# The first piece of wo as loads of 112 and 16 partitions, with the last 6 KB of the 16 in threes

## The chip, the cores and the metric

The kernel runs on one core of a Trainium2 chip. TensorE (PE) multiplies, VectorE (DVE), ScalarE (ACT) and GpSimd (POOL) work beside it, and SyncE (SP) issues most of the transfers between the memory outside (HBM) and the on-chip memory SBUF of 128 partitions. Sixteen DMA engines carry the transfers. The time is the device time of one execution in microseconds (us); comparisons use the median of several executions of each kernel.

## The reference

One token is decoded. Attention with 32 query heads and 8 key heads over a cache of 32768 positions is mixed by a gate with a gated feed-forward block:

```
q = x @ wq                                   # 32 heads of 128
p = softmax(q k^T / sqrt(128)); o = p v      # 8 key heads, 4 queries each, 32768 positions
a = o.reshape(1, 4096) @ wo                  # wo: 4096 x 512
b = (silu(x @ w1) * (x @ w3)) @ w2           # 512 -> 1792 -> 512
out = g * a + (1 - g) * b,   g = sigmoid(sum(x * gate_w))
```

All is float32. The two caches are 128 MB each, so nearly all of the time is their reading.

## The kernel before, in words

Two buffers of 64 KB a partition, big_a and big_b, take the caches turn by turn in units of 8 MB: 16 units of keys, then 16 of values with a lag of four. PE computes scores from transposed keys and products with values, DVE transposes the keys and finds the softmax's maxima and sums, ACT copies a part of each key unit into the tile aside and takes the exponentials.

The order of the work is written out in the program. A small class (Program) keeps, for each engine, a list of operations with the keys that each one reads and writes; from these it works out on which semaphore an operation must wait. The function load (L195) puts a transfer on SP's list. Each such load takes one of nine semaphores in turn (its lane), so a load waits until the load that used the lane nine loads earlier has landed. SP issues its list in order, and all that SP issues stands in one queue (q1) of the 16 DMA engines.

What matters here is the end. The last four units of values are loaded into big_a and big_b (load_unit, L592 to L603), then w2 into the tile aside (L604). As soon as PE has used the third of those units (values at L606), big_a is free, and SP issues wo into it in six pieces (L608 to L610). wo is seen as 128 partitions x 32 rows of 512 numbers: a partition has 32 contiguous rows of 2 KB, 64 KB in all. The six pieces are rows 0 to 16, 16 to 23, 23 to 27, 27 to 29, 29 to 31 and 31 to 32 of every partition, that is 32, 14, 8, 4, 4 and 2 KB a partition.

Meanwhile PE does the last unit of values, DVE folds in w2 by parts (down, L635), and the attention's result is laid out in otp (L644). Then PE multiplies by wo. The first three pieces are used by "wide" products, one group for each piece (L650, recorded at L630), each waiting for its own piece; DVE adds their sum to acc (L652). The last three are used by products of 128 columns (L661), which also take in acc. A copy (L673) and two stores (L504) end the kernel.

Of the kernel before, what the change touches and what calls it, by code (L numbers as in the profile page):

```python
# [13 lines left out]
P = 128  # L14
# [104 lines left out]
def kernel(  # L119
# [13 lines left out]
    nc = tc.nc  # L133
# [23 lines left out]
    pr = Program(nc, tc.alloc_semaphore)  # L157
# [12 lines left out]
    wo_t = big[0].rearrange("p (k e) -> p k e", k=32)  # L170
# [15 lines left out]
    otp = kt[1][:, 0:1024].rearrange("p (k c) -> p k c", c=32)  # L186
# [8 lines left out]
    def load(dst, src, writes, over=()):  # L195
        lanes[0] += 1
        lane = f"load{lanes[0] % 9}"
        return pr.add(
            "SP", lambda: nc.sync.dma_start(dst, src), writes=writes, over=[*over, lane], inc=lane, by=16, also=lane,  # L199
        )  # L200
# [81 lines left out]
    for c in range(NC):  # L282
        def part(c=c):
# [18 lines left out]
         reads=["gate0"], writes=["gate1"])  # L302
# [39 lines left out]
    def window(t, z):  # L342
        return act(
            lambda: A.copy(winc, win[:, t // 4, :, 16 - 16 * z:48 - 16 * z]),  # L344
            reads=[("win", t // 4, r) for r in range(4)], writes=["winc"], credit="windows",
        )
# [162 lines left out]
    first = window(0, 0)  # L509
    for t in range(NH):  # L510
# [9 lines left out]
        if t + 1 < NH:  # L520
            load_keys(t + 1)
            first = window(t + 1, 0)
# [83 lines left out]
        values(7, 0, z, region(0, z), f"A{z}")  # L606
    wod = wo.rearrange("(p k) e -> p k e", k=32)
    parts = ((0, 16), (16, 23), (23, 27), (27, 29), (29, 31), (31, 32))  # L608
    for a, b in parts:
        load(wo_t[:, a:b, :], wod[:, a:b, :], [("wo", a)], over=["A0", "A1"])  # L610


# [13 lines left out]
    def wide(i, ws, **kw):  # L626
        def go():
            for j, (w, t) in enumerate(ws):
                r = 32 * (j % 4)
                ins = T.matmul(pa[r:r + 32, :], w, t, start=(i == 0 and j < 4), stop=(final[j % 4] == (i, j)))  # L630
            return ins
        pe(go, writes=["f0"], **kw)


    def down(ks):  # L635
# [9 lines left out]
        reads=[("each", 0), ("each", 1), "otp"], writes=["lay"])  # L645
# [2 lines left out]
    down(range(3, FR))  # L648
    laid = ["otp", "lay"]
    for i, (a, b) in enumerate(parts[:3]):  # L650
        wide(i, [(otp[:, k, :], wo_t[:, k, :]) for k in range(a, b)], reads=[*laid, ("wo", a)])
    dve(lambda: V.tensor_add(acc, acc, pa), reads=["acc", "f0"], writes=["acc"])  # L652


# [27 lines left out]
    a, b, c, d = flips  # L682
# [67 lines left out]
```

## Time and profile before

| | us |
|---|---|
| time, median of 3 runs | 693.98 (693.81 to 694.11) |
| the profiled execution, from first to last instruction (its span, the one time that the page gives of it) | 692.4 |
| PE busy | 402.8 |
| DVE busy | 368.4 |
| ACT busy | 134.6 |
| data moved by DMA | 296.34 MB at a mean of 428 GB/s |

The profile is of one execution. Its page gives busy times, the span in 40 slices, the DMA queues, and the chain of work that ended last. Further views give the instructions in order of time (the timeline), the list of DMA issues with the time to landing, and, for any stretch of the span, the busy time of each engine, the granted clock of PE, the busy share of the 16 DMA engines and their rate. A DMA's packets are counted by queue; q1 is SP's, q10 is ACT's.

### The profile page before, as it was taken

The page shows a single profiled execution, that of the slowest core. Times are in us where ns is not written, and L with a number is a line of the kernel's source. Part 1 is how long each engine was busy: PE and PEld are TensorE (multiplying, and loading weights), DVE is VectorE, ACT ScalarE, POOL GpSimd, SP SyncE. Part 2 cuts the span into 40 slices and gives each one's busy share as a digit, 9 for nine tenths or more (in the row PEclk, how much of TensorE's full clock was granted, in tenths as well). Part 3 has the DMA queues.
Part 4 walks back from the last instruction along what each step waited for, and adds up shares of the span by engine and source line. Part 5 has one row for each costly group of instructions (what it writes and reads, how often), then busy time and mean ns, then how long its engine had stood idle before and what let it go on. Part 6 is the DMA issues. An engine that isn't in the chain of part 4 may idle for free. (4 is left out here: it accounts for less than half of the span.)

```text
span 692.4 us, 5704 instructions
## 1 busy us (share of the span) xinstructions
PE 402.8 (58%) x2430; PEld 94.6 (14%) x2430; DVE 368.4 (53%) x229; ACT 134.6 (19%) x113; POOL 8.1 (1%) x34
## 2 busy tenths in 40 slices
PE   1537777566474656557484645666573646744575
PEld 0101111201010110201010101201010102211121
DVE  0049999394735637493726537593826546700026
ACT  0143223232303130220303131210303131100000
POOL 4000000000000000000000000000000000000000
PEclk9969999958667676977786777778586777776689
DMA  9999999999999999999999999999999999999996
GB/s 386 455 428 424 424 424 436 448 443 424 428 428 428 435 454 432 424 432 428 432 454 435 424 428 428 432 435 451 432 424 428 428 435 454 435 421 424 433 421 284
DMA packets 6068, 296.34 MB, mean 428 GB/s; under 512 B 678, under 2 KB 682, under 8 KB 1068
## 3 DMA queue, kind: packets, MB, share of 16 engines
q1 hardware_dynamic: 6052, 296.23, 99.1%
q8 instruction: 5, 0.08, 0.0%
q14 instruction: 3, 0.02, 0.0%
q10 hardware_dynamic: 8, 0.01, 0.0%
HBM read 296.23 MB, written 0.00 MB: 428 GB/s over the span
## 5 line engine op out<-in xcount | busy, mean ns | idle before, releaser
L366 DVE STREAM_TRANSPOSE aside<-big_a 128x2048 f32<-128x2048 f32 x41 | 94.3, 2300 | 166.9 <-DMA big_a<-in_A_k_cache_dram 166.9
L350 PE MATMUL ps<-aside,winc 128*32 128x512 f32 x512 | 96.0, 830 | 142.4 <-PEq L688 141.5
L350 PE MATMUL ps<-kt,winc 128*32 128x512 f32 x512 | 96.2, 832 | 61.2 <-PEq L688 61.2
L451 PE MATMUL ps<-big_b,pv 128*32 128x512 f32 x768 | 96.1, 657 | 17.5 <-PEq L688 17.5
L338 ACT COPY aside<-big_a 128x6144 f32<-128x6144 f32 x14 | 74.4, 5313 | 151.8 <-DMA big_a<-in_A_k_cache_dram 151.8
L366 DVE STREAM_TRANSPOSE kt<-aside 128x2048 f32<-128x2048 f32 x32 | 73.4, 2293 | 17.2 <-PE ps L350 17.2
L366 DVE STREAM_TRANSPOSE kt<-big_a 128x2048 f32<-128x2048 f32 x28 | 63.5, 2269 | 0.0
L379 ACT COPY sb<-ps 128x512 f32<-128x512 f32 x16 | 17.1, 1069 | 156.8 <-PE ps L350 156.8
L350 PEld LDWEIGHTS ps<-aside,winc 128*32 128x32 f32 x512 | 13.4, 125 | 215.7 <-issue 215.7
L451 PEld LDWEIGHTS ps<-big_b,pv 128*32 128x32 f32 x768 | 27.7, 120 | 88.1 <-issue 88.1
L366 DVE STREAM_TRANSPOSE aside<-aside 128x2048 f32<-128x2048 f32 x16 | 36.3, 2269 | 0.0
L583 DVE TENSOR_TENSOR sb<-ps,own_b 128x512 f32<-128x512 f32 x2 | 1.4, 691 | 60.8 <-PE ps L574 60.8
L350 PEld LDWEIGHTS ps<-kt,winc 128*32 128x32 f32 x512 | 13.3, 123 | 143.8 <-issue 143.8
L574 PE MATMUL ps<-big_b,probs 128*32 128x512 f32 x128 | 18.0, 726 | 18.8 <-DMA big_b<-in_A_v_cache_dram 18.8
L344 ACT COPY winc<-win 128x128 f32<-128x128 f32 x32 | 9.8, 306 | 78.7 <-PE ps L350 78.7
L574 PE MATMUL ps<-big_a,probs 128*32 128x512 f32 x128 | 17.3, 703 | 10.1 <-DMA big_a<-in_A_v_cache_dram 10.1
L614 PE MATMUL ps<-win,ones 128*128 128x512 f32 x42 | 22.7, 635 | 0.0
L366 DVE STREAM_TRANSPOSE aside<-big_b 128x2048 f32<-128x2048 f32 x7 | 16.0, 2291 | 11.4 <-DMA big_b<-in_A_k_cache_dram 11.4
L262 PE MATMUL ps<-acc 128*128 128x512 f32 x34 | 20.0, 670 | 2.5 <-POOL acc L219 1.6
L400 DVE TENSOR_REDUCE mt<-turned 128x8 f32<-128x2048 f32 x4 | 9.2, 2291 | 22.6 <-PE turned L389 22.6
L424 DVE TENSOR_REDUCE sums<-probs 128x8 f32<-128x2048 f32 x4 | 15.2, 3801 | 2.1 <-ACT probs L417 2.1
L288 PE MATMUL turned<-big_a,xp 128*32 128x512 f32 x64 | 8.5, 691 | 12.1 <-DMA big_a<-in_A_wq_dram 12.1
(93 smaller groups left out, 186.6 us busy)
## 6 DMA issues: line engine op xcount, KB each, us to landing
big_b<-in_B_w_dram SPq DMA_DIRECT2D x2, 3584.0 KB, 20.8
big_a<-in_A_wo_dram SPq DMA_DIRECT2D x1, 4096.0 KB, 27.6
aside<-in_B_w_dram SPq DMA_DIRECT2D x1, 3584.0 KB, 37.4
big_a<-in_A_wo_dram SPq DMA_DIRECT2D x1, 1792.0 KB, 31.5
big_a<-in_A_wo_dram SPq DMA_DIRECT2D x1, 1024.0 KB, 33.5
big_a<-in_A_wo_dram SPq DMA_DIRECT2D x2, 512.0 KB, 34.7
big_a<-in_A_wo_dram SPq DMA_DIRECT2D x1, 256.0 KB, 35.2
big_a<-in_A_k_cache_dram SPq DMA_DIRECT2D x14, 26.3
```

Of the source, the lines that this page charges most:

```text
L262: return T.matmul(ps_s, acc[:, 0:P], acc, start=True, stop=False, skip_group_check=True)
L288: ins = T.matmul(pf[b][32 * j:32 * j + 32, :], xp[:, c, :], t[:, o:o + REP * DH], start=(c == 0), stop=(c == NC - 1),)
L338: act(lambda: A.copy(spare, src[:, :, 32:128]), reads=[key], writes=["wo"])
L344: lambda: A.copy(winc, win[:, t // 4, :, 16 - 16 * z:48 - 16 * z]),
L350: ins = T.matmul(ps_s[32 * g:32 * g + 32, :], winc[:, c, :], kt[c % 2][:, 512 * g:512 * g + 512], start=False, stop=False, skip_group_chec ...
L366: k = dve(lambda d=dst, s=src: V.transpose(d, s), reads=[key], writes=[f"kt{c % 2}"], over=["kt0"] * (t >= LAG and (z, c) == (1, 1)), cred ...
L379: lambda: A.copy(sb[:, :, :, t % 4], ps_s.rearrange("p (n i) -> p n i", i=32)),
L400: dve(lambda: V.tensor_reduce(mt[:, 0:8], turned.rearrange("p (n q) -> p q n", q=8), axis=AX.X, op=ALU.max), reads=banks, writes=["mt"])
L424: dve(lambda: V.tensor_reduce(sums[:, 8 * w:8 * w + 8].rearrange("p (u q) -> p u q", u=2), probs[:, :, 0:1024].rearrange("p u (n q) -> p u ...
L451: ins = T.matmul(ps_o[32 * t:32 * t + 32, :], pv[:, o:o + 32], big[1][:, n * P:(n + 4) * P], start=((z, g) == (0, 0)), stop=((z, g) == (1, ...
L574: ins = T.matmul(ps_o[32 * t:32 * t + 32, :], prob[u][:, o:o + 32], vt[:, n * P:(n + 4) * P], start=((e, z, g) == (0, 0, 0)), stop=((e, z, ...
L614: return T.matmul(bank[:, 0:n], ones, win.rearrange("p w c n -> p (w c n)")[:, 0:n], start=True, stop=True)
```

## The change

The first of the six pieces (32 KB of all 128 partitions) is issued as eight loads: 26 KB of the partitions 112 to 127; then the remaining 6 KB of these 16 partitions as five loads of three partitions and one of one; then 32 KB of the partitions 0 to 111. The eight loads count up one semaphore, named first, by 16 each. The first group of wide products waits for all eight. The five other pieces are issued as before.

```
     parts = ((0, 16), (16, 23), (23, 27), (27, 29), (29, 31), (31, 32))
-    for a, b in parts:
+    top_rows, split = 112, 13
+    pieces = [(top_rows, P, 0, split)]
+    pieces += [(p, min(p + 3, P), split, 16) for p in range(top_rows, P, 3)]
+    pieces += [(0, top_rows, 0, 16)]
+    first = [("wo", 0, i) for i in range(len(pieces))]
+    for key, (p, q, a, b) in zip(first, pieces):
+        pr.add("SP", lambda p=p, q=q, a=a, b=b: nc.sync.dma_start(wo_t[p:q, a:b, :], wod[p:q, a:b, :]),
+               writes=[key], over=["A0", "A1"], inc="first", by=16)
+    for a, b in parts[1:]:
         load(wo_t[:, a:b, :], wod[:, a:b, :], [("wo", a)], over=["A0", "A1"])
...
     for i, (a, b) in enumerate(parts[:3]):
-        wide(i, [(otp[:, k, :], wo_t[:, k, :]) for k in range(a, b)], reads=[*laid, ("wo", a)])
+        landed_keys = [("wo", a)] if i else first
+        wide(i, [(otp[:, k, :], wo_t[:, k, :]) for k in range(a, b)], reads=[*laid, *landed_keys])
```

## The prediction

> **What bounds the kernel now.** I read the page first, then the chain of waits, the timeline of the last 60 us, the list of DMA issues, and last the stretches around the end. The page:
>
> ```profile
> span 692.4 us, 5704 instructions
> ...
> DMA  9999999999999999999999999999999999999996
> ...
> DMA packets 6068, 296.34 MB, mean 428 GB/s; under 512 B 678, under 2 KB 682, under 8 KB 1068
> ...
> q1 hardware_dynamic: 6052, 296.23, 99.1%
> ...
> q10 hardware_dynamic: 8, 0.01, 0.0%
> ```
>
> The 16 DMA engines are busy in every slice but the last, at 428 GB/s, and one queue (q1, all that SP issues) carries 99.1% of it. The kernel is a stream of 296 MB; what is worth anything must move the end of that stream. The end of the chain says the same (start, length, what):
>
> ```profile
> 641.79 9.86 PE ps L574 x64
> 651.65 0.02 issue
> 651.67 0.33 SPq L199
> ...
> 653.46 35.07 DMA big_a<-in_A_wo_dram
> 688.53 0.04 issue
> 688.58 1.10 PE turned L661 x24
> ```
>
> PE frees the buffer at 651.65, SP then issues the pieces of wo, and PE waits for them. The timeline shows how little follows:
>
> ```profile
> 632.09 0.43 SPq L199 DMA_DIRECT2D aside<-in_B_w_dram  x1
> ...
> 651.67 2.70 SPq L199 DMA_DIRECT2D big_a<-in_A_wo_dram  x6
> ...
> 661.07 8.71 PE L574 MATMUL ps<-big_b,probs 128*32 128x512 f32 x64 [9.46 <-DMA big_b<-in_A_v_cache_dram]
> ...
> 679.39 3.64 PE L630 MATMUL turned<-big_a,kt 128*32 128x512 f32 x32 [3.17 <-DMA big_a<-in_A_wo_dram]
> ...
> 683.59 1.92 PE L630 MATMUL turned<-big_a,kt 128*32 128x512 f32 x14 [0.56 <-DMA big_a<-in_A_wo_dram]
> ...
> 689.21 0.16 PEld L661 LDWEIGHTS turned<-big_a,kt 128*32 128x32 f32 x8 [0.25 <-DMA big_a<-in_A_wo_dram]
> ...
> 689.70 0.29 DVE L673 COPY winc<-turned 128x128 f32<-128x128 f32 x1 [1.80 <-PE turned L661]
> ...
> 690.02 0.33 SPq L504 DMA_DIRECT2D out_dram<-winc  x1
> ```
>
> The last piece of wo lets PE go at 689.2. From there to the end of the span are 3.2 us of fixed work (eight matmuls, a copy, the store). So the question is when the last engine delivers its last bytes. The stretches around that moment, with the share of the 16 DMA engines that is busy and the rate as the last two columns:
>
> ```profile
> 685.80:686.20 0.40, 0.12 (x4) 0.12 (x8) 0.00 (x0) 0.00 (x0) 0.00 (x0) 1.00 1.00 394
> 686.20:686.60 0.40, 0.40 (x8) 0.04 (x6) 0.00 (x0) 0.00 (x0) 0.00 (x0) 1.00 0.87 333
> 686.60:687.00 0.40, 0.40 (x8) 0.00 (x0) 0.00 (x0) 0.00 (x0) 0.00 (x0) 1.00 0.60 236
> 687.00:687.40 0.40, 0.20 (x8) 0.06 (x8) 0.18 (x1) 0.00 (x0) 0.00 (x0) 1.00 0.35 143
> 687.40:687.80 0.40, 0.40 (x16) 0.32 (x16) 0.40 (x1) 0.00 (x0) 0.00 (x0) 1.00 0.38 149
> 687.80:688.20 0.40, 0.40 (x16) 0.16 (x8) 0.10 (x1) 0.00 (x0) 0.00 (x0) 1.00 0.36 138
> 688.20:688.60 0.40, 0.21 (x12) 0.03 (x4) 0.00 (x0) 0.00 (x0) 0.00 (x0) 1.00 0.12 46
> 688.60:689.00 0.40, 0.40 (x16) 0.35 (x16) 0.00 (x0) 0.00 (x0) 0.00 (x0) 1.00 0.01 5
> ```
>
> This is the view that matters. All 16 engines run until 686.2; by about 687.0 ten of them have finished, 0.35 to 0.38 of 16, that is six, go on to 688.2, and the last one ends just past 688.6. Every engine has the same bytes, so **ten are early and six late by 1 to 2 us**, and the late ones set the end. No view says which six.
>
> **How a load is cut.** The packets tell. SP issues 42 loads of 128 rows and one store of two rows. 42 times (128 rows + 16 marks of completion) plus (2 + 2) is 6052, the count of q1. ACT's queue has two loads of one row and one store of two: 2 x (1 + 1) + (2 + 2) = 8, the count of q10. So a row is one packet, and there are as many marks, one for each engine that takes part, as the row count allows: 16, 2, 1. A load of 112 or 16 rows can be dealt to 16 engines, one of three rows to three. Its rate comes from the issues:
>
> ```profile
> big_a<-in_A_wo_dram SPq DMA_DIRECT2D x1, 4096.0 KB, 27.6
> aside<-in_B_w_dram SPq DMA_DIRECT2D x1, 3584.0 KB, 37.4
> big_a<-in_A_wo_dram SPq DMA_DIRECT2D x1, 1792.0 KB, 31.5
> ```
>
> The first piece lands at 651.67 + 27.6 = 679.27, the second (issued at 652.04 by the chain) at about 683.55: 4.3 us for the 112 KB of each engine, 0.0384 us per KB. So 6 KB are 0.23 us, a row of 26 KB 1.00, a row of 32 KB 1.23.
>
> **The change part by part.**
>
> *Bytes per engine.* Before, the first piece is 8 rows x 32 KB = 256 KB for each engine. After, each has 26 KB (one of the 16 rows) + 7 x 32 KB = 250 KB: 6 KB less, **-0.23 us** for all 16. The 16 ends of 6 KB that are left go out in threes: five rows for each of three engines, +5 x 0.23 = +1.15, net **+0.92**; the single row gives one of them another 0.23, net **+1.15**. Six more completion marks cost little (678 packets under 512 B come to nothing visible beside 0.99 busy); I add 0.05. Whether the five loads fall on the same three engines no row shows. Bounds: dealt on and on they would come out even, one row each, and the sum is 0; on the same three it is as above. I take the same three, because every load of the trace begins its dealing anew (each leaves whole eighths, with nothing to carry on). [...]
>
> *Where that leaves the end.* If all three are among the ten early ones: the latest of these ends at about 687.0, plus 1.2 is 688.2, still before 688.7 - 0.23 = 688.5. The end moves by **-0.23**. If one is among the six late ones: these end between 688.1 and 688.7, plus 0.97 to 1.2 gives 689.0 to 689.9, against 688.7: **+0.3 to +1.2**. By counting alone all three are early with 10/16 x 9/15 x 8/14 = 0.21. I take **+0.3**, the near edge of the second case, beside the first.
>
> *SP's queue.* Six issues took 2.70 us, 0.45 each; the first piece now takes eight instead of one, so seven more, 3.2 us, and SP is done at 657.5 instead of 654.4. Nothing waits for that: ahead of wo in the same queue stand the last unit of v (PE gets it at 661.07) and w2 (632.09 + 37.4 = 669.5), so the engines reach wo 12 us later. SP's next work is the store at 690.02. Without that cover the issues would cost their 3.2 us. The five later pieces slide by one lane in the ring of nine semaphores; the loads whose lanes they take over landed before 651, so no wait is added there.
>
> *PE's wait.* The first 16 wide products waited for one load, now for eight on one semaphore (128). Behind that wait stand all later products of L630 and L661. The wait ends when the slowest of the 16 engines is through its part, as now; a delay of 1.2 would start the first group at 680.6, and its 3.64 us end at 684.2, before the second piece (683.55 + 1.2 = 684.75). PE stays behind the transfers. DVE's sums beside it are not touched.
>
> **What no row prices: 16 engines writing 16 neighbouring rows.** Every load in the trace but two tiny ones covers 128 rows. If the way into SBUF is private to an engine, the load of 16 rows takes 1.00 us as worked out above, and the price is 0. If n engines must share a way for neighbouring rows, it takes n x 1.00, and all else in the queue stands behind it. The ends are n = 1 (0) and n = 16 (+15); from n = 2.6 on the loss is over 1.6 us, past what a measurement can tell from no change (0.2%, 1.39 us). The load of 112 rows has the same trouble in small: with seven rows each, two engines can meet on one way in each of the seven steps, from 0 to 7 x 1.23 = +8.6. For the forecast I take the lower end, n = 1: the nearest rows are the loads of 128, which run at the full rate of 16 engines. Both ends stay for the range.
>
> **The rivals.**
>
> 1. *Shared ways into SBUF (slower).* Place: the load of 16 rows, then that of 112. Price with n = 4, the middle of 1 and 16 by ratio: +3.0, and half of 8.6 for the 112 rows, +4.3, less 0.2: **+7.1, 701.1**; its ends are +1.4 and +11.4. For it: all rows of this program's loads are dealt in full sets of 128, the only form seen at full rate. Against it: nothing in the trace shows an engine slowed by another. [...]
> 2. *Balance as it may be meant (-0.23, 693.75).* All three engines are early. For it: ten of 16 are. Against it: the count of 0.21. It is the lower part of my forecast.
> 3. *The change does not do what it says (0, 693.98).* The rows go to engines by partition, or the three-row loads are dealt round: each engine has its old 256 KB and the end stays. For it: no view names engines.
> 4. *Hidden gain above 0.2%.* Would need 1.4 us off the six late engines; the change takes 0.23. Only if the split itself changed who is late.
>
> **How the numbers follow.** The profile's span is 692.4; the runs' median of 693.98 has 1.6 more around it, and I carry changes over one to one. Chances: bytes shifted among engines without a price for ways (my forecast, -0.23 to +1.2, rival 2 in it) 0.45; rival 3 0.10; rival 1 0.42; rival 4 0.03. The predicted time is 693.98 + 0.3 = **694.3**, and that case's own range 693.6 to 695.3. All of it lies within 0.2% (692.6 to 695.4). So faster 0.03, same 0.55, slower 0.42. The range goes from 693.5 to **703.5**, which takes in rival 1 up to +9.5 of its 11.4 and leaves out some 0.1 above, and about 0.05 below.
>
> **What would show it.** The packets of q1: 144 for the first piece become (16 + 16) + 5 x (3 + 3) + (1 + 1) + (112 + 16) = 192, so 6100 in all; another count says that the loads are cut otherwise. The shares by stretch: in the forecast the DMA engines stay at 0.95 or more from 669 to 686, and one to three engines run on alone up to 1.2 us longer at the end. Under rival 1 the rate falls well under 400 GB/s while the 16 rows and the 112 rows are written, the first group of wide products starts at 682 or later instead of 679.4, and all that follows slides by as much. SP's 13 issues should take about 5.9 us and end near 657.5, with no one waiting. The prediction is wrong if the first group starts more than 1.5 us late, or if PE waits for SP.

## The result, and the profile after

The change makes the kernel slower. The median goes from 693.98 us (693.81 to 694.11) to 706.68 (705.08 to 708.81), five executions of each, a ratio of 1.018 with a 95% interval of 1.017 to 1.019, or +12.7 us. The forecast was 694.3, and its range ended at 703.5. The page of the profile after (that execution took 705.83):

```profile
span 704.1 us, 5711 instructions
...
DMA  9999999999999999999999999999999999999996
GB/s 414 418 417 432 458 400 441 448 432 424 424 458 424 421 443 443 424 424 454 424 424 436 447 424 424 451 432 424 425 451 428 421 443 443 422 424 451 374 222 243
DMA packets 6116, 296.34 MB, mean 421 GB/s; under 512 B 710, under 2 KB 714, under 8 KB 1116
...
q1 hardware_dynamic: 6100, 296.23, 99.1%
```

The packets of q1 are the 6100 that the prediction asked for, which fits loads cut as it said: 112 and 16 rows over 16 engines, three rows over three. What is new stands in the slices: the last three fall to 374, 222 and 243 GB/s (433, 421 and 284 before), and **in the row above them the DMA engines still show a 9**, but for the very last slice, in which the kernel ends. The engines are not waiting for work. By this count they hold a packet each and are slow with it. The span grew by 11.7 us, nearly all that the median grew. The end of the chain (start, length, what):

```profile
651.50 0.34 SPq L615
...
653.79 37.39 DMA big_a<-in_A_wo_dram
691.18 0.14 issue
691.32 8.07 PE turned L638 x48
699.41 0.70 DVE acc L661
700.11 0.04 issue
700.15 1.25 PE turned L670 x32
```

The timeline of the same execution:

```profile
651.50 2.61 SPq L615 DMA_DIRECT2D big_a<-in_A_wo_dram  x8
654.15 2.32 SPq L199 DMA_DIRECT2D big_a<-in_A_wo_dram  x5
...
673.11 2.33 DVE L645 SCALAR_TENSOR_TENSOR acc<-aside,htp,acc 128x512 f32<-128x512 f32 x3 [1.67 <-DMA aside<-in_B_w_dram]
...
691.32 8.03 PE L638 MATMUL turned<-big_a,kt 128*32 128x512 f32 x54 [15.26 <-DMA big_a<-in_A_wo_dram]
...
700.93 0.16 PEld L670 LDWEIGHTS turned<-big_a,kt 128*32 128x32 f32 x8 [0.19 <-DMA big_a<-in_A_wo_dram]
701.43 0.29 DVE L682 COPY winc<-turned 128x128 f32<-128x128 f32 x1 [1.33 <-PE turned L670]
```

SP needed 5.0 us for its 13 issues and was done at 656.5, so it delayed nobody. The first group of wide products started at 691.3 instead of 679.4: 11.9 us late, the whole loss. DVE's first step with w2 is late too: 673.11 instead of 671.52, where no wait for a transfer stood before:

```profile
671.52 2.32 DVE L637 SCALAR_TENSOR_TENSOR acc<-aside,htp,acc 128x512 f32<-128x512 f32 x3
```

Now it waits for w2's landing. The list of issues gives w2, which stands before wo in the queue,

```profile
aside<-in_B_w_dram SPq DMA_DIRECT2D x1, 3584.0 KB, 41.2
```

41.2 us after its issue instead of 37.4. That is no chance of one execution: in the kernels below with loads of 64, 32 and 16 neighbours DVE waits for w2 as well (1.07, 2.63 and 1.97 us, until 672.76, 673.84 and 673.59), and in the three whose first load covers all 128 partitions it starts between 670.86 and 671.94 with no such wait. The reading, which no view shows engine by engine: engines that were already through with w2 and wrote the first rows of wo slowed down engines that were not. The stretches of 3 us from the moment at which the engines reach wo, after the change (the last two columns are the busy share of the DMA engines and GB/s):

```profile
666.60:669.60 3.00, 3.00 (x33) 0.65 (x21) 0.00 (x0) 0.00 (x0) 0.00 (x0) 1.00 1.33 203
669.60:672.60 3.00, 2.18 (x9) 0.87 (x6) 1.71 (x2) 0.00 (x0) 0.00 (x0) 1.00 0.97 181
672.60:675.60 3.00, 3.00 (x9) 1.19 (x7) 2.42 (x4) 0.00 (x0) 0.00 (x0) 1.00 0.99 212
675.60:678.60 3.00, 0.45 (x2) 0.00 (x0) 2.96 (x3) 0.00 (x0) 0.00 (x0) 1.00 0.85 208
678.60:681.60 3.00, 0.00 (x0) 0.00 (x0) 2.87 (x4) 0.00 (x0) 0.00 (x0) 0.96 0.98 251
681.60:684.60 3.00, 0.00 (x0) 0.00 (x0) 2.86 (x5) 0.00 (x0) 0.00 (x0) 0.50 1.17 284
684.60:687.60 3.00, 0.00 (x0) 0.00 (x0) 1.79 (x3) 0.00 (x0) 0.00 (x0) 0.50 0.79 181
687.60:690.60 3.00, 0.00 (x0) 0.00 (x0) 0.00 (x0) 0.00 (x0) 0.00 (x0) 0.50 0.92 233
```

and the first two of the same stretches before:

```profile
666.60:669.60 3.00, 3.00 (x32) 0.72 (x24) 0.00 (x0) 0.00 (x0) 0.00 (x0) 1.00 1.07 460
669.60:672.60 3.00, 2.18 (x8) 0.78 (x5) 2.67 (x4) 0.00 (x0) 0.00 (x0) 1.00 0.95 399
```

For 24 us the queue moves 181 to 284 GB/s, 219 on the mean, with a mean share of one: half of the 428 of before, while the engines count as busy. (A share above 1 comes from counting a packet wholly in the stretch in which it starts.) PE's clock falls from 0.96 to 0.50 while PE has nothing to do (0.00 busy from 678.6 to 690.6), and its 54 wide products then take 8.0 us, where they took 6.6 before, so PE stands last in the chain. That costs nothing more here: the last piece was issued near 656.1 and took 44.8 us to land, so it was there at 700.9, when PE still waits for it (the line at 700.93), 0.5 ahead of the last copy at 701.43, as it was before (689.2 and 689.70).

### The profile page after: what moved, and what is told of

The parts are those of the page before. It is cut to its first block, busy times and chain, and to the rows that moved or that the text cites. A ratio compares the mean times of both kernels' runs of the same rounds, so it can differ in the third digit from the quotient of the medians.

```text
span 704.1 us, 5711 instructions
## 1 busy us (share of the span) xinstructions
PE 399.5 (57%) x2430; PEld 95.3 (14%) x2430; DVE 368.5 (52%) x229; ACT 134.7 (19%) x113; POOL 8.1 (1%) x34
## 5 line engine op out<-in xcount | busy, mean ns | idle before, releaser
L350 PE MATMUL ps<-kt,winc 128*32 128x512 f32 x512 | 93.4, 809 | 62.0 <-PEq L697 62.0
L638 PE MATMUL turned<-big_a,kt 128*32 128x512 f32 x54 | 8.0, 742 | 15.3 <-DMA big_a<-in_A_wo_dram 15.3
## 6 DMA issues: line engine op xcount, KB each, us to landing
aside<-in_B_w_dram SPq DMA_DIRECT2D x1, 3584.0 KB, 41.2
big_a<-in_A_wo_dram SPq DMA_DIRECT2D x1, 256.0 KB, 44.8
```

Source lines behind the costliest of these rows:

```text
L350: ins = T.matmul(ps_s[32 * g:32 * g + 32, :], winc[:, c, :], kt[c % 2][:, 512 * g:512 * g + 512], start=False, stop=False, skip_group_chec ...
```

## The experiments

Four theories stood against each other at first. **Shared ways** is rival 1 of the prediction. It supposes that in a load of 128 no engine slows another, and that in other loads n engines at a time meet on a way into SBUF and share the rate of one. No view shows a way or names an engine, and n = 4 for 16 neighbours was the author's choice. **A price per load**: eight loads in place of one. **The engines that carry the threes** set the end. **The reading side**: the order of the rows read from HBM sets the rate. The kernels of this section differ from the changed one only in the loads of the first piece, which still use the one semaphore. After the first edit only the lines put in are shown.

**The same piece as loads of 64, 32 and 16 neighbours.** The edit, with 64, 32 or 16:

```
-    top_rows, split = 112, 13
-    pieces = [(top_rows, P, 0, split)]
-    pieces += [(p, min(p + 3, P), split, 16) for p in range(top_rows, P, 3)]
-    pieces += [(0, top_rows, 0, 16)]
+    each_load = 64
+    pieces = [(p, p + each_load, 0, 16) for p in range(0, P, each_load)]
```

> The first piece of wo as two loads of 64 neighbouring partitions, 32 KB each, all else as in the changed kernel. [...] Theory of a price per load: the changed kernel's eight loads cost 12.7, so each load beyond the first 1.8: +1.8, about 695.8. Theory of the reading side (the rows' addresses in memory outside set the rate): two halves of the same contiguous 8 MB, no reason for a loss: 694.

> The first piece as four loads of 32 neighbouring partitions. [...] Price per load: three more loads, +5.4, about 699.4. Reading side: between the loads of 64 and of 16, no figure of its own.

> The first piece as eight loads of 16 neighbouring partitions. [...] Price per load: as many loads as the changed kernel, so +12.7, about 706.7.

Measured beside a kernel before of 693.9: 706.7 for 64 (ratio 1.018, 1.017 to 1.020), 707.1 for 32 (1.019, 1.018 to 1.021), 714.3 for 16 (1.030, 1.028 to 1.031). Two loads cost as much as four, and as much as the changed kernel's eight, while another eight cost 20.4. A price per load is out. One stretch of each, of 64, 32 and 16:

```profile
682.00:688.00 6.00, 0.00 (x0) 0.00 (x0) 3.97 (x6) 0.00 (x0) 0.00 (x0) 0.50 0.88 183
```
```profile
682.00:688.00 6.00, 0.00 (x0) 0.00 (x0) 4.99 (x7) 0.00 (x0) 0.00 (x0) 0.50 0.89 182
```
```profile
676.00:682.00 6.00, 0.23 (x1) 0.00 (x0) 5.82 (x7) 0.00 (x0) 0.00 (x0) 0.71 0.95 150
```

Again engines that are busy, at less than half of 428 GB/s on the mean: over the three stretches of 6 us from 670 to 688 the loads of 64 have 183, 229 and 183 GB/s, those of 32 have 188, 229 and 182, those of 16 have 153, 150 and 175. Loads of 32 and 64 neighbours cost nearly the same, 13.2 and 12.8, and those of 16 cost more, 20.4. That is the direction of shared ways. The sizes are not: the piece has eight rows of 1.23 us for each engine, so half rate throughout would cost another 9.8, where 12.8 and 13.2 were measured, and n = 4 throughout would cost three times as much, 29.5, where 20.4 was. Loads of 16 follow each other in the queue, and an engine that is through with one goes on to the next, so the same four engines need not meet throughout. That explanation is argued, not measured.

**Without the threes.**

```
+    top_rows = 112
+    pieces = [(top_rows, P, 0, 16), (0, top_rows, 0, 16)]
```

> The first piece as two loads, partitions 112 to 127 and 0 to 111, 32 KB each: the five loads of three partitions and the one of one are gone. Shared ways: the load of 16 takes 4 x 1.23 instead of 1.23, and the load of 112 stays as slow as in the changed kernel, whose loss it hardly changes: 705 to 708. Price per load: one load more than before, +1.8, about 695.8. Theory that the engines which carry the threes set the end: the loss of 12.7 is nearly all gone, 694 to 697.

706.9 (1.019, 1.017 to 1.020): the loss stays. The engines that carry the threes do not make it.

**Which end of the transfer: write or read.** With near = 16 neighbours and far = 16 partitions eight apart, each of the eight loads writes one kind and reads the other (the second run exchanges the two in zip):

```
+    near, far = [slice(16 * i, 16 * i + 16) for i in range(8)], [slice(i, P, 8) for i in range(8)]
+    pieces = list(zip(near, far))
...
+    for key, (to, at) in zip(first, pieces):
+        pr.add("SP", lambda to=to, at=at: nc.sync.dma_start(wo_t[to, 0:16, :], wod[at, 0:16, :]),
```

> The first piece as eight loads of 16, written into 16 neighbouring partitions, but read from rows of wo that lie eight partitions apart (so wo's rows stand in another order, and the output is that of another matrix). Shared ways into SBUF: only the place written to counts, four engines on a way as in the loads of 16 neighbours, so 714 again (712 to 716). Reading side: what is read decides, and it is the same as in the twin that writes far and reads near only if addresses do not matter; then this one differs from 714 by more than 3 and goes with the other order of reading.

> The twin: eight loads of 16 written into partitions eight apart, read from 16 neighbouring rows (again another order of wo's rows). [...] Reading side: it reads what the loads of 16 neighbours read, so 714.

Written near and read far: 716.1 (712.2 to 719.6; ratio 1.034, 1.031 to 1.036). Written far and read near: 707.1 (1.019, 1.017 to 1.021). The written side decides: written near goes with the loads of 16 neighbours (714.3), written far with those of 32 and 64. Reading in another order adds 1.8 us to the median (716.1 against 714.3), within the 7 us over which those four executions spread.

**The load of 112 alone.**

```
+    top_rows = 112
+    pieces = [(0, top_rows, 0, 16)]
```

> The first piece as one load of partitions 0 to 111, 32 KB each; the 32 KB of partitions 112 to 127 are not loaded at all (their share of the product is missing). If the load of 112 is slow by itself, two engines meeting on a way in a part of its steps: its loss without that of the load of 16 and with one row less for each engine, 701 to 704. If the loss came from the load of 16 neighbours alone: seven rows instead of eight at full rate, 1.2 us less than before, 692.8.

702.2 (1.012, 1.010 to 1.014). Its timeline has the first group of wide products at

```profile
687.27 8.27 PE L636 MATMUL turned<-big_a,kt 128*32 128x512 f32 x54 [11.36 <-DMA big_a<-in_A_wo_dram]
```

With seven rows for each engine at full rate this kernel would take 693.8 - 1.2 = 692.6. So **the load of 112 alone costs 9.6 us**. The load of 16 without threes brings 706.9 - 702.2 = 4.7 instead of the 1.23 of a row of 32 KB, 3.8 times as much, close to the n = 4 of rival 1. The load of 16 with the threes brings 4.5. While the load of 112 is written, this kernel's stretches show the same picture as the loads of 64:

```profile
676.00:679.00 3.00, 0.00 (x0) 0.00 (x0) 2.89 (x5) 0.00 (x0) 0.00 (x0) 1.00 0.87 208
679.00:682.00 3.00, 0.00 (x0) 0.00 (x0) 2.86 (x5) 0.00 (x0) 0.00 (x0) 0.87 0.93 211
```

The five stretches of 3 us from 670 to 685 have 218, 300, 208, 211 and 212. That is 230 on the mean, about half of 428, as if two engines shared the rate of one in nearly every step. Which side sets it was tested on loads of 16 and not on this one, so for the load of 112 the meeting is argued from its rate.

**Is it meeting, or being away from home?** If the rows of a load are dealt in order, which no view shows, an engine of the load of 112 also writes partitions that a load of 128 would not give it. Loads of 8 partitions four apart were to take meeting away; that they would was the author's assumption:

```
+    at = [64 * h + 32 * s + j for h in range(2) for s in range(2) for j in range(4)]
+    pieces = [(slice(p, p + 29, 4),) * 2 for p in at]
```

The packets fit eight engines for a load of 8: 16 x (8 + 8) in place of the changed kernel's 192 make 6164 in q1, as counted. Each of the eight then has 16 rows, at 1.22 us a row 19.5 us for the piece where 16 engines take 9.8. So if no engine slows another, the end moves by 9.8 to 703.6, and the first group of wide products from 679.4 to 689.2.

> [...] The first eight loads go to partitions 0 to 63, the others to 64 to 127. [...] Theory of home ways: an engine is slow whenever it writes outside the partitions that a load of 128 gives it, shared or not; then the second half, which the same eight engines write, takes 2.3 us a row instead of 1.22, 8 x 1.1 = 8.6 more: about 712, with the first group at about 696.

704.9 (1.016, 1.015 to 1.018), and the stretches show why it is 11 slower than before and no more:

```profile
667.00:675.00 8.00, 7.18 (x44) 2.29 (x37) 4.31 (x6) 0.00 (x0) 0.00 (x0) 1.00 1.00 421
...
683.00:691.00 8.00, 1.24 (x8) 0.45 (x12) 2.55 (x4) 0.00 (x0) 0.00 (x0) 0.50 0.49 209
691.00:699.00 8.00, 7.69 (x78) 2.38 (x74) 0.69 (x1) 0.00 (x0) 0.00 (x0) 0.84 0.43 180
```

First all 16 engines run at full rate (421 GB/s at a share of 1.00), by this reading eight of them on the first piece, the rest on later pieces. Then half of the engines are done, and the share is 0.49: 7.8 engines carry 209 GB/s, 26.8 each, the rate of an engine before (428 / 16). By then they write partitions 64 to 127. If the same eight wrote 0 to 63, they are away from home in one half or the other, and neither of the two stretches shows them slowed (the one between, 241 GB/s at 0.67, has 22.5 for each busy engine). The first group began at 689.76, near the 689.2 of engines that do not slow each other and far from the 696 of home ways. The twin with 8 neighbours differs in the spacing alone (of what it writes and of what it reads):

```
+    pieces = [(slice(p, p + 8),) * 2 for p in range(0, P, 8)]
```

> The twin of the loads of 8 partitions four apart: 16 loads of 8 neighbouring partitions, the same bytes, the same number of loads and of engines (8), only the spacing differs. [...] A price per load, per engine or for addresses gives the twin's 704.9.

724.0 (1.043, 1.036 to 1.051; two executions, 721.8 and 726.2), 19 more than the twin, and a stretch in which only eight engines work:

```profile
691.00:699.00 8.00, 0.00 (x0) 0.00 (x0) 0.00 (x0) 0.00 (x0) 0.00 (x0) 0.50 0.50 123
```

The same number of loads, bytes and engines as in the twin, but 123 GB/s in place of 209. The direction is that of shared ways: with the spacing alone changed, the rate falls. Eight engines at 123 GB/s are 15 each, a bit over half of 26.8. How many of them meet, and how they spread over loads that follow each other, no view of the profile shows.

**The threes by themselves.** A floor (26 KB of all 128 partitions, the rest left out), then the floor with the threes, then the floor with one load of 16 rows of 6 KB, one edit after the other:

```
+    pieces = [(0, P, 0, split)]
...
+    pieces += [(p, min(p + 3, P), split, 16) for p in range(top_rows, P, 3)]
...
+    pieces = [(0, P, 0, 13), (top_rows, P, 13, 16)]
```

> A floor for the next two: the first piece is one load of all 128 partitions, 26 KB each; the other 6 KB of each partition are not loaded (rows 13 to 15 of every partition are missing from the product). Every engine carries 8 x 6 = 48 KB less at 0.0384 us per KB: 1.84 us less than before, about 692.0, by every theory.

> As the floor (26 KB of all 128 partitions), and then the last 6 KB of partitions 112 to 127 in five loads of three and one of one; the last 6 KB of the other 112 partitions are missing. This is the step of the change that was to relieve 13 engines, without the loads of 112 and of 16. If an engine's way is its own: three engines carry 5 x 0.23 = 1.15 more, one of them 1.4; over the floor by 0 to 1.4, so 692.0 to 693.4. [...]

> As the floor, and then the last 6 KB of partitions 112 to 127 as one load of 16 (one row for each engine); the last 6 KB of the other 112 partitions are missing. Way of its own: 0.23 over the floor, 692.2. Shared ways, four engines on each: 4 x 0.23 = 0.92 over the floor, about 692.9, less what the engines' different arrivals spread out.

The floor is 691.9 (ratio 0.997, 0.996 to 0.998), as expected. With the threes it is 693.3 (0.999, 0.998 to 1.000), 1.3 over the floor, near the upper end of the 0 to 1.4 that an engine with a way of its own allows, so this pair alone does not speak against such a way. With the one load of 16 it is 693.2 (0.999, 0.998 to 1.000), also 1.3 over the floor, far from the 0.2 of an own way and above even the 0.9 of n = 4. Handing the 16 ends to three engines is worth nothing against handing them to 16 (693.3 and 693.2).

## Why the prediction was wrong

What held: the view of the bound (the end of the stream sets the end), the count of packets, SP's queue (hidden; 0.38 an issue instead of 0.45), PE's wait (no new work behind it), and the bytes of each engine, whose price per KB the floor confirmed (1.9 measured, 1.84 reckoned).

**The step that failed** is the price of nothing for the loads of 16 and of 112: "For the forecast I take the lower end, n = 1: the nearest rows are the loads of 128, which run at the full rate of 16 engines." Those rows could not carry that choice. Every large load of the trace had all 128 partitions, so they could show neither that a way is private nor that it is shared; they only show 428 GB/s in loads of 128. With 3.8 times the price of a row measured for the load of 16 (4.7 against 1.23), and 9.6 instead of 0 for the load of 112, the loss follows.

**Rival 1 had the right place and direction as far as the runs test it, and its sum was too small**: +7.1 against +12.7. Its n = 4 was a choice that no run of the kernel before shows; the runs put the 3.8 for the load of 16 in its place, and no run shows a way itself. The load of 16 was sized well (+3.0 for its 26 KB, and 4.7 - 1.2 = 3.5 measured for 32 KB). The load of 112 was not: "half of 8.6" was a choice between ends, and the run gives 9.6, above the upper end of 8.6. That end took two engines to a way in each of seven steps, which is half rate; loads of part of the partitions ran a little under it here (4 MB as loads of 64 took 12.8 more where half rate is 9.8). Why under half is open. The range stopped short too: its top lay at +9.5, below the +11.4 that rival 1 was given, and the measured +12.7 is above both.

That the loads of threes all fall to the same three engines was the author's choice, and no view names an engine. The loads of 8 speak for it as far as they can: with a share of 0.49 and 0.50 half of the engines stay idle through loads that come one after another, so the same eight seem to be taken each time; which eight no view shows.

The shift of bytes among engines, which was the forecast's own matter (-0.23 to +1.2), can't be seen beneath a loss of 12.7. The floor with the threes has +1.3 over the floor, which less the 0.23 of relief would be +1.1, near the upper end of that range; but one load of 16 costs as much there, and no run showed the relief of 0.23 by itself.

## What to carry to other kernels

A load's shape decided more here than its bytes per engine: cutting 128 partitions into 112 and 16, or into halves, left the DMA engines busy (a mean share of 1.00 and 0.94) and the rate at about half (219 and 198 GB/s instead of 428). So judge a stream by the rate beside the busy share, not by the share alone. And where a trace holds only one form of an operation, that form is no evidence on another; price the new form by the mechanism that it brings in, or keep the range open up to its far end.

## What the runs showed of the hardware

Loads of 32 and of 64 neighbouring partitions lost nearly the same (+13.2 and +12.8 us over 4 MB), loads of 16 more (+20.4). In loads of 16 it is where they write that decided and not where they read (716.1 and 707.1 for the same two sets of rows with the sides exchanged). At half the engines busy (shares of 0.49 and 0.50) loads of 8 carried 209 GB/s into partitions four apart and 123 into neighbours. And a slow load reached back in its queue: w2, issued before it, took 41.2 us to land instead of 37.4. Open is how the engines of a load of 112 meet, if they do, since no view names the engine of a packet.
